# A later first sum of the second routing search, a small load ahead of the token gathers, and a token's place as the smaller of two positions

## Chip, cores, metric

One Trainium2 chip, one of its NeuronCores. The metric is device time of one execution in microseconds (us); lower is better.

## What is computed

Three parts follow one another: windowed attention over 4 x 576 tokens with 8 heads, a mixture-of-experts layer whose router gives each of the 8 experts exactly 288 of the 2304 tokens, and a second layer in which every token goes through all 8 experts, weighted by a balanced (Sinkhorn) table. Cut to what matters here:

```python
def _moe_ref(x, w_gate, w1, w2):
    cap = N // E                                   # 2304 // 8 = 288
    logits = x @ w_gate
    order = np.argsort(-logits.flatten())          # best (token, expert) pairs first
    for idx in order:
        tok, e = (int(idx) // E, int(idx) % E)
        if assigned[tok] >= 0 or counts[e] >= cap:
            continue
        assigned[tok] = e
        counts[e] += 1
    for e in range(E):
        mask = assigned == e
        out[mask] = np.maximum(x[mask] @ w1[e], 0.0) @ w2[e]

def _moe2_ref(x, w_gate, w1, w2):
    P = sinkhorn(np.exp(x @ w_gate - max))         # 8 rounds of row and column sums
    return sum(P[:, e:e + 1] * (np.maximum(x @ w1[e], 0.0) @ w2[e]) for e in range(E))
```

## The kernel before, in words

The program is written in the order in which each engine runs it; waits between engines are put in by the framework. Float32 matrices are split into a high and a low float16 half, and three products (high-high, high-low, low-high) stand for one.

**Routing.** The greedy assignment is done in eight searches (`Router.phase`, one per expert that fills up). A search finds the threshold at which some expert reaches its 288 tokens, six digits of it one after the other. A digit takes these steps: VectorE compares all tokens' scores with up to 64 candidate values (tile `G`, line 504, in two halves); TensorE sums the comparison over the 128 partitions in 18 thin matmuls (line 576); VectorE compares the sums with the room left (`ok`, line 585); TensorE makes a count of `ok` (line 588, "the sum of the digit"); VectorE takes the largest (`cur`, line 590) and forms the next candidates. The search ends in the chosen tokens (`ze`, lines 606 and 607), in an index for the expert's weight rows (`widx`, line 615), in the positions of the chosen tokens (two matmuls, lines 618 and 619, with all-ones and with a triangular matrix `tri`; a running sum `pos`, line 621), and in a list of token numbers: `hot`, two halves of one-hot comparisons (line 640, also named `G` in the trace), 18 thin matmuls (line 671), `idx` (line 676). `books` (lines 654 to 660) takes the filled expert and its tokens out of the scores; line 683 counts what every expert has used.

**Gathers.** `fetched` (GpSimd's queue) gathers the expert's first-layer weight rows by `widx` (line 868), then its 288 token rows from the DRAM tensor `xd` by `idx` into the tile `xg` (line 877, three DMAs), then the second-layer weights. ScalarE makes the high half (line 847) and VectorE the low half (line 838, "the split"). The first layer's splits are called `w1l`, the second layer's `w2l` in the trace; other tiles share these names, so lines tell them apart.

**Main work of stage 1.** For each of the eight experts: transposes of the gathered tokens (line 922), first layer (`l1`, line 907, 8 tiles of 12 matmuls of 288 columns), second layer (line 948, 4 tiles of 24 matmuls; after each, ScalarE and VectorE take it out, lines 952 to 966, which I call the tile's batch), then expert 0 of the second mixture for the tokens so far (`m2_l1`, 96 matmuls of 256 columns, and `m2_l2`). After expert 1 on, a small gate product (`gate2`, line 1287) stands between the second layer and `m2_l1`.

**How searches and main work are laced.** `interleave` runs the main generator and hands over to the search when the nanoseconds that the main work has announced reach what the search asked for (`need`). The search's `yield 1900` is such a request. The first search runs alone, ahead of any expert, with throw-away matmuls (`warm`, line 808) between its digits. The second search is started before the lacing begins: its first digit's comparisons and 18 sums are issued, and the first request of the lacing, `need=1900`, decides where its count (line 588) stands among the first expert's matmuls. Every later request counts from there, so all later places in stage 1 hang on this number.

**Stage 2** (the second mixture's experts 1 to 7) is a long stretch of matmuls that this change does not touch.

Lines of the rows and of the order below are those of the kernel before where the order is of before; in the changed kernel the same statements stand one line higher or up to five lower.

Of the kernel before, what the change touches and what calls it, by code (L numbers as in the profile page):

```python
# [11 lines left out]
F32 = mybir.dt.float32  # L12
F16 = mybir.dt.float16
# [3 lines left out]
OP = mybir.AluOpType  # L17
AX = mybir.AxisListType

B, H, S, D = 4, 8, 576, 64  # L20
N, DM, E, F = 2304, 512, 8, 1024
CAP = N // E
# [356 lines left out]
NC = NT  # L379
STEPS = [6, 5, 5, 5, 5, 6]  # L380
COUNT = 0x4B000000


def step_constants():
# [3 lines left out]
    for n, w in enumerate(STEPS):  # L388
# [9 lines left out]
        if n > 1:  # L398
            u ^= np.uint32(COUNT << (shift + w) & 0xFFFFFFFF)
        out.append(u)  # L400
# [6 lines left out]
def route_tables():  # L407
    p = np.arange(128)
    f = {}
    f["tri"] = -(p[:, None] > p[None, :]).astype(np.float32)  # L410
    c = np.arange(NC)
    base = 128 * c
    val = np.zeros((128, NC, 2), np.float32)
    val[:, :, 0] = base // 64
    val[:, :, 1] = p[:, None]
    f["val"] = val.reshape(128, -1)
    f["iota"] = np.tile(np.arange(1, QB + 1, dtype=np.float32), (128, 1))
    f["code"] = np.tile(8.0 - np.arange(E, dtype=np.float32), (128, 1))
    f["group"] = np.tile(np.arange(3, dtype=np.float32), (128, 1))
    f["wa"] = np.tile(np.array([-DM] * 4 + [-F] * 8, np.float32), (128, 1))  # L420
    f["wb"] = np.concatenate([8 * DM + 128 * np.arange(4)[None] + p[:, None],
                              8 * F + 128 * np.arange(8)[None] + p[:, None]], 1).astype(np.float32)
    cols, n = {}, 0
    for k, a in f.items():
        cols[k] = (n, a.shape[1])
        n += a.shape[1]
    return cols, np.concatenate(list(f.values()), 1)


RC, RTAB = route_tables()  # L430


class Router:
# [96 lines left out]
    def phase(self, ph):  # L530


        nc, wk, Lm = self.nc, self.wk, self.Lm
        V = nc.vector
# [5 lines left out]
        ze = wk.tile([128, 2 * NC], F16, name="ze")  # L540
        if not last:
# [10 lines left out]
            for n, bits in enumerate(STEPS):  # L552
# [7 lines left out]
                elif n:  # L560
                    x = wk.tile([128, 64], I32, name="x")[:, :T]
                    V.scalar_tensor_tensor(x, cur.bitcast(I32).to_broadcast([128, T]), left, base,
                                           op0=OP.logical_shift_left, op1=OP.bitwise_xor)
# [5 lines left out]
                p = self.psum()  # L569
# [7 lines left out]
                if n:  # L577
# [4 lines left out]
                    else:  # L582
                        V.tensor_scalar(base, x[:, 0:1], COUNT, None, op0=OP.bitwise_xor)
                ok = wk.tile([64, E], BF, name="ok")[:T]
# [16 lines left out]
            up = wk.tile([128, NC], F32, name="up")  # L601
# [14 lines left out]
        p = self.psum()  # L616
# [1 line left out]
        nc.tensor.matmul(p[:, :2 * NC], self.ones, ze, start=True, stop=True)  # L618
        nc.tensor.matmul(p[:, 64:64 + 2 * NC], self.tri, ze, start=True, stop=True, skip_group_check=True)
        pos = wk.tile([128, 2 * NC], F32, name="pos")  # L620
        V.tensor_tensor_scan(out=pos, data0=self.one_f, data1=p[:, :2 * NC], initial=0.0, op0=OP.mult, op1=OP.add)
        zv = wk.tile([128, 2 * NC], F32, name="zv")
        V.tensor_add(pos, pos, p[:, 64:64 + 2 * NC])
        V.scalar_tensor_tensor(zv, pos, CAP + 0.5, ze, op0=OP.is_le, op1=OP.mult)
        V.tensor_mul(pos, pos, zv)
        r = wk.tile([128, NC], F32, name="r")
        V.tensor_add(r, pos[:, :NC], pos[:, NC:])
        g = wk.tile([128, NC], F32, name="g")
        V.tensor_scalar(g, r, QB + 0.5, None, op0=OP.is_ge)
        V.scalar_tensor_tensor(g, r, 2 * QB + 0.5, g, op0=OP.is_ge, op1=OP.add)  # L630
# [22 lines left out]
        def books():  # L653
            V.scalar_tensor_tensor(GA, bc(m), cur, A, op0=OP.is_gt, op1=OP.mult)
            V.tensor_scalar(ng, code, wx, -1e30, op0=OP.is_equal, op1=OP.mult)
            V.tensor_sub(self.left, self.left, wx)
            V.tensor_scalar(up, m, cur, -100.0, op0=OP.is_gt, op1=OP.mult)
            V.tensor_add(self.mask, self.mask, up)
            V.scalar_tensor_tensor(self.mask, zv[:, NC:], -100.0, self.mask, op0=OP.mult, op1=OP.add)
            V.tensor_add(Lm, Lm, be(ng))  # L660

        if not last:
# [4 lines left out]
        p = self.psum()  # L667
# [29 lines left out]
SLACK, SL2 = 0.7, 1.06  # L697


def interleave(main, side, slack=lambda: 1.0, drain=True, need=0.0):  # L700


    room = 0.0
    for ns in main:
        room += ns
        while side is not None and room >= need:
            need = next(side, None)
            room = 0.0
            if need is None:
                side = None  # L710
            else:
                need *= slack()
    if side is not None and drain:
        for _ in side:
            pass


class Moe:
# [610 lines left out]

    def stage1(self, ctx, late):  # L1330

        pool = lambda n, b: ctx.enter_context(self.tc.tile_pool(name=n, bufs=b, side="right"))
        x2 = pool("m_x2", 1)
        self.x2 = [x2.tile([128, KT, 2, HN], F16, name="x2" + c) for c in "hl"]
        for i, need in enumerate(self.r.phase(0)):
            if need > 2000:
                self.warm(2)
            if i in (2, 4):
                late.pop(0)()
            if i == 8:  # L1340
                self.load_gate2()

        def routes():
            for ph in range(1, E):
                self.ph = ph
                yield from self.r.phase(ph)
# [9 lines left out]
        side = routes()  # L1356
# [48 lines left out]
                            yield from self.moe1_x(ready)  # L1405
                        yield ns

        interleave(main(), side, lambda: SLACK if self.ph == 1 else SL2, need=1900)

        def last():  # L1410
            x = self.xp.tile([128, 2 * KT, CAP], F16, name="xt", bufs=1).rearrange("p a b -> p (a b)")
# [98 lines left out]
```

## Time and profile before

| what | value |
|---|---|
| runs of the kernel before | 1759.36, 1760.49, 1765.73 us, median 1760.49 us |
| the profiled execution | 1749.37 us |
| its span, first to last instruction | 1747.6 us |
| VectorE busy | 1341.5 us (77%) |
| ScalarE busy | 846.3 us (48%) |
| GpSimd busy | 238.6 us (14%) |
| mean granted TensorE clock over the span | 0.988 |
| chain that ended last | TensorE 61%, issue 10%, VectorE 5%, ScalarE 2% |

PE is TensorE's matmuls, PEld its weight loads, DVE VectorE, ACT ScalarE, POOL GpSimd, SP the engine that issues plain DMAs. A time in brackets at the end of a row is how long the engine had been idle before the instruction, with the engine, tile and line whose end released it; "issue" means that nothing the profile shows was waited for. A clock of 1.00 is 2.4 GHz, 0.50 is 1.2 GHz.

### The profile page before, as it was taken

How to read it: one execution, taken by the hardware profiler on the slowest of the kernel's cores; microseconds unless marked ns; L12 is line 12 of the kernel's file. 1: busy time of each engine (PE TensorE's matmuls, PEld its weight loads, DVE VectorE, ACT ScalarE, POOL GpSimd, SP SyncE). 2: the span in 40 equal slices, each digit the busy share in tenths (PEclk: the TensorE clock that was granted, in tenths of full speed). 3: DMA queues.
4: the chain of work that ended last, by engine and by line, in shares of the span. 5: the costliest groups of instructions: out<-in, count | busy, mean ns of one | idle time of the engine just before them, and what ended most of it. 6: DMA issues, size and time to landing. Idle time of an engine off the chain costs nothing.

```text
span 1747.6 us, 34883 instructions
## 1 busy us (share of the span) xinstructions
PE 1709.8 (98%) x14326; PEld 1280.6 (73%) x14326; DVE 1341.5 (77%) x2572; ACT 846.3 (48%) x1544; POOL 238.6 (14%) x293
## 2 busy tenths in 40 slices
PE   9978999999999999999999999999999999999998
PEld 7956677767777577777777777777777777777777
DVE  6977777766647888878887887888788878886656
ACT  7833443334444455644445543565445544454433
POOL 1323333223410000000000000000000000000111
PEclk9977999999999999999999999999999999999999
DMA  9923444332733144343435235432544334433120
GB/s 330 279 59 110 124 125 134 95 98 77 213 99 102 76 163 154 137 159 112 176 127 209 88 138 211 155 130 89 201 161 157 123 131 155 165 138 148 37 100 37
DMA packets 107568, 241.19 MB, mean 138 GB/s; under 512 B 46384, under 2 KB 72496, under 8 KB 100496
## 3 DMA queue, kind: packets, MB, share of 16 engines
q1 hardware_dynamic: 86768, 151.64, 25.0%
q0 software_dynamic: 20384, 87.05, 14.3%
q8 instruction: 112, 1.84, 0.4%
q14 instruction: 48, 0.39, 0.1%
q10 hardware_dynamic: 256, 0.28, 0.1%
HBM read 173.64 MB, written 61.73 MB: 135 GB/s over the span
## 4 chain that ended last, share of the span: by engine, by line
PE 61%; issue 10%; DVE 5%; ACT 2%; POOL 1%; DMA 0%; POOLq 0%; ACTq 0%; DVEq 0%
PE mm L1176 27%; PE mm L1214 25%; PE mm L907 4%; PE mm L992 3%; PE mm L948 1%; DVE hl L1133 1%; POOL out_dram L1228 1%; ACT raw L1045 0%; DVE w1l L1048 0%; DVE r L1048 0%; DMA raw<-in_w2a_dram,widx 0%; DVE w2l L966 0%; PE r L576 0%; ACT hh L1132 0%; DVE xg L913 0%
## 5 line engine op out<-in xcount | busy, mean ns | idle before, releaser
L1176 PE MATMUL mm<-xb,w1h 128*128 128x384 f16 x2352 | 573.3, 326 | 1.3 <-DVE mm L1147 0.8
L1214 PE MATMUL mm<-w2h,hh 128*128 128x256 f16 x1764 | 480.8, 273 | 0.4 <-DVE t L1238 0.2
L1214 PE MATMUL mm<-w2l,hh 128*128 128x256 f16 x1764 | 480.8, 273 | 0.0
L1214 PE MATMUL mm<-w2h,hl 128*128 128x256 f16 x1764 | 480.8, 273 | 0.0
L1176 PE MATMUL mm<-xb,w1l 128*128 128x384 f16 x1176 | 383.3, 326 | 0.0
L1214 PEld LDWEIGHTS <-hh 128*128 128x128 f16 x3528 | 345.2, 98 | 43.0 <-issue 0.9
L1176 PEld LDWEIGHTS <-w1h 128*128 128x128 f16 x2352 | 230.0, 98 | 154.7 <-issue 6.6
L1214 PEld LDWEIGHTS <-hl 128*128 128x128 f16 x1764 | 172.6, 98 | 20.1
L1133 DVE TENSOR_TENSOR hl<-r,hh 128x1536 f16<-128x1536 f32 x84 | 147.5, 1756 | 41.2 <-ACT hh L1132 41.2
L1176 PEld LDWEIGHTS <-w1l 128*128 128x128 f16 x1176 | 115.0, 98 | 76.1
L1128 ACT ACTIVATE r<-mm 128x384 f32<-128x384 f32 x252 | 119.1, 481 | 100.5 <-PE mm L1176 100.5
L1094 POOL DMA_DIRECT2D ws<-raw x48 | 26.0, 541 | 928.6 <-ACT raw L1045 660.4
L1132 ACT ACTIVATE hh<-r 128x1536 f16<-128x1536 f32 x84 | 124.6, 1483 | 43.6 <-DVE r L1157 41.6
L1139 ACT ACTIVATE mm<-mm 128x384 f32<-128x384 f32 x84 | 40.3, 479 | 175.3 <-PE mm L1176 175.3
L1133 DVE TENSOR_TENSOR hl<-S,hh 128x1152 f16<-128x1152 f32 x84 | 113.5, 1351 | 0.0
L1224 DVE SCALAR_TENSOR_TENSOR acc<-t,P,acc 128x512 f32<-128x512 f32 x126 | 94.7, 752 | 4.5
L907 PE MATMUL mm<-xt,w1h 128*128 128x288 f16 x512 | 97.5, 290 | 0.0
L1132 ACT ACTIVATE hh<-S 128x1152 f16<-128x1152 f32 x84 | 96.4, 1147 | 0.4 <-DVE S L1161 0.4
L1045 ACT ACTIVATE raw<-raw 128x1024 f16<-128x1024 f32 x48 | 50.6, 1055 | 87.3 <-DVE raw L1029 45.8
L912 ACT ACTIVATE w1h<-mm 128x288 f16<-128x288 f32 (+1 forms) x120 | 46.9, 396 | 88.1 <-PE mm L907 87.9
L913 DVE SCALAR_TENSOR_TENSOR w1l<-mm,w1h 128x288 f16<-128x288 f32 (+1 forms) x120 | 50.0, 435 | 45.4 <-ACT w1h L912 45.3
L868 POOL DMA_INDIRECT raw<-in_w2a_dram,widx x64 | 75.9, 1186 | 55.3 <-issue 20.4
(265 smaller groups left out, 2921.5 us busy)
## 6 DMA issues: line engine op xcount, KB each, us to landing
xb<-xw SPq DMA_DIRECT2D x30, 1344.0 KB, 5.9
ws<-raw POOLq DMA_DIRECT2D x48, 448.0 KB, 3.3
ws<-r POOLq DMA_DIRECT2D x48, 448.0 KB, 3.0
raw<-in_w2b_dram SPq DMA_DIRECT2D x32, 512.0 KB, 4.4
raw<-in_w1b_dram SPq DMA_DIRECT2D x56, 256.0 KB, 9.0
w1h<-ws SPq DMA_DIRECT2D x6, 1792.0 KB
w1l<-ws SPq DMA_DIRECT2D x6, 1792.0 KB
w2h<-ws SPq DMA_DIRECT2D x6, 1792.0 KB, 7.2
```

Source lines behind the costliest of these rows:

```text
L868: self.nc.gpsimd.indirect_dma_start(out=r[:, i, :], out_offset=None, in_=rows[lay], in_offset=bass.IndirectOffsetOnAxis(ap=widx[:, c:c + 1 ...
L907: nc.tensor.matmul(p, a[:, k, 128 * f:128 * (f + 1)], rhs(k, b), start=(done[f] == 1 and i == 0), stop=(done[f] == KT and i == 2), skip_gr ...
L912: nc.scalar.activation(h[0][:, f, :n], p, AF.Relu)
L913: nc.vector.scalar_tensor_tensor(h[1][:, f, :n], p, 0.0, h[0][:, f, :n], op0=OP.max, op1=OP.subtract)
L992: nc.tensor.matmul(p, a[:, f, c], b[:, f, :], start=(f == 0 and n == 0), stop=(f == FT - 1 and n == 2))
L1045: self.nc.scalar.activation(hi[:, k], x, AF.Copy, scale=sw)
L1128: nc.scalar.activation(o, p, AF.Relu, scale=SH)
L1132: yield nc.scalar.activation(hq[0][:, i, k], x, AF.Copy)
L1133: yield V.tensor_sub(hq[1][:, i, k], x, hq[0][:, i, k])
L1176: nc.tensor.matmul(p, w[u][:, 2 * j + i // 2, k, 128 * (i % 2):128 * (i % 2 + 1)], x[:, v, r, j], start=(q in (1, 5) and j == 0 and n == 0 ...
L1214: nc.tensor.matmul(p, h[u][:, i, a, 128 * t:128 * (t + 1)], w[v][:, i, b, :], start=(q in (1, 7) and i == 0 and j == 0), stop=(q in (2, 3) ...
L1224: V.scalar_tensor_tensor(self.acc[:, r, :], x, self.P[:, r, e:e + 1], self.acc[:, r, :], op0=OP.mult, op1=OP.add)
```

## The change

Three edits.

- **Place.** `tri` gets -1000 on its diagonal and the running sum starts at 1000, so that a token that isn't chosen has a position above 1000 and a chosen one its own. The place is then the smaller of the two positions (assigned and tied), and two VectorE operations that masked the positions (`zv` and a product) go. In `books`, the mask that used `zv` takes two operations in place of one.
- **Load.** At the seventh step of the first search a DMA on GpSimd's queue reads 38 x 2 single elements of `xd`, spread over the last batch's rows, into a tile `near` that nobody reads. In the built program this load carries the waits for the eight queues of the DMAs that wrote `xd`; the first token gather (line 877) waited for eleven semaphores before, and waits for three after.
- **First request.** `need` goes from 1900 to 3300.

```diff
 def route_tables():
-    f["tri"] = -(p[:, None] > p[None, :]).astype(np.float32)
+    f["tri"] = -(p[:, None] > p[None, :]).astype(np.float32) - FAR * np.eye(128, dtype=np.float32)
...
-        V.tensor_tensor_scan(out=pos, data0=self.one_f, data1=p[:, :2 * NC], initial=0.0, op0=OP.mult, op1=OP.add)
-        zv = wk.tile([128, 2 * NC], F32, name="zv")
+        V.tensor_tensor_scan(out=pos, data0=self.one_f, data1=p[:, :2 * NC], initial=FAR, op0=OP.mult, op1=OP.add)
         V.tensor_add(pos, pos, p[:, 64:64 + 2 * NC])
-        V.scalar_tensor_tensor(zv, pos, CAP + 0.5, ze, op0=OP.is_le, op1=OP.mult)
-        V.tensor_mul(pos, pos, zv)
         r = wk.tile([128, NC], F32, name="r")
-        V.tensor_add(r, pos[:, :NC], pos[:, NC:])
+        V.tensor_tensor(r, pos[:, :NC], pos[:, NC:], op=OP.min)
...
-            V.scalar_tensor_tensor(self.mask, zv[:, NC:], -100.0, self.mask, op0=OP.mult, op1=OP.add)
+            V.tensor_scalar(up, pos[:, NC:], CAP + 0.5, -100.0, op0=OP.is_le, op1=OP.mult)
+            V.tensor_add(self.mask, self.mask, up)
...
+            if i == 6:
+                near = self.xp.tile([38, 2], F16, name="near", bufs=1)
+                xd = self.xd
+                nc.gpsimd.dma_start(near, bass.AP(tensor=xd.tensor, offset=xd.offset + S * (B - 1) * 2 * DM,
+                                                  ap=[[30 * DM, 38], [DM, 2], [1, 1]]))
...
-        interleave(main(), side, lambda: SLACK if self.ph == 1 else SL2, need=1900)
+        interleave(main(), side, lambda: SLACK if self.ph == 1 else SL2, need=3300)
```

What the last edit does to the order, at three places.

TensorE, at the start of the first expert, before. `xg` are the gathered tokens that are transposed, `count` the first sum of the second search, `zero` a throw-away matmul:

```order
L922 LDWEIGHTS xg
L922 MATMUL mm<-id_102,xg 128x96
L588 LDWEIGHTS count
L588 MATMUL r<-ok,count 128x8
L808 LDWEIGHTS zero
L808 MATMUL mm<-zero 128x512
```

The same count in the changed kernel, twelve first-layer matmuls (one tile) later:

```order
L906 LDWEIGHTS w1l
L906 MATMUL mm<-xt,w1l 128x288
L589 LDWEIGHTS count
L589 MATMUL r<-ok,count 128x8
L906 LDWEIGHTS w1h
L906 MATMUL mm<-xt,w1h 128x288
```

The count moved from between the last transpose and the throw-away matmuls to behind the first tile; the later counts of this search follow at the same distances as before (18, then 12 matmuls with the 18 thin sums between), each one tile later.

VectorE, second and third digit of the second search, before. `ok` is the comparison that the digit's count waits for; `w2l<-raw` are the splits of the first expert's second-layer weights, of which there are four, and one stands ahead of the rows shown:

```order
L590 TENSOR_REDUCE cur<-r 128x1
L562 SCALAR_TENSOR_TENSOR x<-cur,base 128x32
L504 TENSOR_TENSOR G<-m,x 128x288 x2
L913 SCALAR_TENSOR_TENSOR w1l<-mm,w1h 128x288
L838 SCALAR_TENSOR_TENSOR w2l<-raw,w2h 128x1024
L581 TENSOR_TENSOR base<-thr,x 128x32
L585 TENSOR_TENSOR ok<-r,rem 32x8
L913 SCALAR_TENSOR_TENSOR w1l<-mm,w1h 128x288
L838 SCALAR_TENSOR_TENSOR w2l<-raw,w2h 128x1024 x2
```

The same place in the changed kernel (two splits stand ahead of it):

```order
L591 TENSOR_REDUCE cur<-r 128x1
L563 SCALAR_TENSOR_TENSOR x<-cur,base 128x32
L505 TENSOR_TENSOR G<-m,x 128x288 x2
L912 SCALAR_TENSOR_TENSOR w1l<-mm,w1h 128x288
L837 SCALAR_TENSOR_TENSOR w2l<-raw,w2h 128x1024 x2
L582 TENSOR_TENSOR base<-thr,x 128x32
L586 TENSOR_TENSOR ok<-r,rem 32x8
```

The third digit's `ok` stood ahead of the third and fourth split and stands now behind all four.

VectorE, end of the second search, before. `G<-md,iota` are the two halves of `hot`, the rows of lines 953 and 958 belong to the third tile of the second layer:

```order
L632 SCALAR_TENSOR_TENSOR md<-g,r 128x18
L953 SCALAR_TENSOR_TENSOR x2l<-mm,x2h 128x2x144
L958 TENSOR_TENSOR w1h<-w2l,mm 128x144
L640 TENSOR_TENSOR G<-md,iota 128x864
L645 TENSOR_TENSOR gm<-g,group 128x54
L647 TENSOR_TENSOR rhs<-val,gm 128x108
L640 TENSOR_TENSOR G<-md,iota 128x864
L654 SCALAR_TENSOR_TENSOR w<-m,cur,A 128x144
```

The same in the changed kernel:

```order
L638 TENSOR_TENSOR G<-md,iota 128x864
L643 TENSOR_TENSOR gm<-g,group 128x54
L645 TENSOR_TENSOR rhs<-val,gm 128x108
L952 SCALAR_TENSOR_TENSOR x2l<-mm,x2h 128x2x144
L959 TENSOR_TENSOR w1h<-mm,w1h 128x144
L960 TENSOR_TENSOR w1l<-mm,w2l 128x144
L961 TENSOR_TENSOR w1l<-mm,w1h 128x144
L965 SCALAR_TENSOR_TENSOR w2l<-w1h,w2h 128x2x144
L965 SCALAR_TENSOR_TENSOR w2l<-w1l,w2h 128x2x144
L638 TENSOR_TENSOR G<-md,iota 128x864
L652 SCALAR_TENSOR_TENSOR w<-m,cur,A 128x144
```

The third tile's rows now stand ahead of the positions, and the fourth tile's batch, which stood behind `books`, stands between the two halves of `hot`. In the third to seventh search every part moves by 9 to 12 matmuls in the same direction: the batch of the second tile goes ahead of `pos`, and line 671 stands behind 18 `m2_l1` matmuls where it stood behind 9.

## Rows read from the trace of the kernel before

**Rows 1.** The page, part 1: busy time, share and instructions of each engine.

```profile
PE 1709.8 (98%) x14326; PEld 1280.6 (73%) x14326; DVE 1341.5 (77%) x2572; ACT 846.3 (48%) x1544; POOL 238.6 (14%) x293
```

**Rows 2.** Windows, PE: length, busy (count), granted clock, DMA share, GB/s.

```profile
149.00:149.50 0.50, 0.50 (x9) 0.70 0.65 107
...
230.00:240.00 10.00, 8.89 (x120) 1.00 0.61 177
```

**Rows 3.** Timeline, end of the first search: start, duration, engine, line, operation.

```profile
128.84 1.20 POOL L868 DMA_INDIRECT raw<-in_w1a_dram,widx  x1 [23.19 <-DVE widx L615]
...
129.24 0.20 DVE L624 SCALAR_TENSOR_TENSOR zv<-pos,ze 128x36 f32<-128x36 f32 x1
...
133.86 0.16 DVE L676 SCALAR_TENSOR_TENSOR idx<-s 96x3 int32<-96x3 f32 x1
...
134.90 0.93 POOL L877 DMA_INDIRECT xg<-xd,idx  x1 [0.98 <-ACT w1h L847]
```

**Rows 4.** Timeline, start of the first expert.

```profile
138.99 4.62 DVE L838 SCALAR_TENSOR_TENSOR w1l<-raw,w1h 128x1024 f16<-128x1024 f32 x4
...
141.43 0.82 PE L922 MATMUL mm<-id,xg 96*128 96x96 f16 x8 [0.18 <-DMA xg<-xd,idx]
...
143.74 0.16 PE L588 MATMUL r<-ok,count 64*128 64x8 bf16 x1 [1.49 <-DVE ok L585]
...
145.08 0.69 PE L907 MATMUL mm<-xt,w1h 128*128 128x288 f16 x2
```

**Rows 5.** Timeline, first layer of the first expert and the splits of its second-layer weights.

```profile
149.36 0.77 PE L576 MATMUL r<-A,G 128*128 128x8 f16 x18
...
155.07 1.06 ACT L847 ACTIVATE w2h<-raw 128x1024 f16<-128x1024 f32 x1 [0.58 <-DMA raw<-in_w2a_dram,widx]
155.12 2.34 DVE L838 SCALAR_TENSOR_TENSOR w2l<-raw,w2h 128x1024 f16<-128x1024 f32 x2
...
156.06 0.17 PE L588 MATMUL r<-ok,count 32*128 32x8 bf16 x1
```

**Rows 6.** Waits of PE from 145 to 600 us: total, times, longest.

```profile
PE r L683 <- DVE P L1287: 5.6, 5, 1.1
...
PE r L618 <- DVE ze L607: 1.2, 1, 1.2
PE r L576 <- DVE G L504: 1.0, 2, 0.7
...
PE r L671 <- DVE G L640: 0.6, 1, 0.6
PE mm L907 <- DVE x2l L953: 0.5, 1, 0.5
```

**Rows 7.** Timeline, end of the third search (the second expert's second layer).

```profile
221.49 0.17 DVE L590 TENSOR_REDUCE cur<-r 128x1 f32<-128x8 f32 x1 [2.17 <-PE r L588]
...
223.02 0.45 DVE L953 SCALAR_TENSOR_TENSOR x2l<-mm,x2h 128x288 f16<-128x288 f32 x1
...
224.21 0.23 DVE L621 TENSOR_TENSOR_SCAN pos<-one_f,r 128x36 f32<-128x36 f32 x1
...
225.88 0.45 DVE L953 SCALAR_TENSOR_TENSOR x2l<-mm,x2h 128x288 f16<-128x288 f32 x1
...
227.87 1.05 DVE L640 TENSOR_TENSOR G<-md,iota 128x864 f16<-128x864 f16 x1
...
229.26 0.45 DVE L953 SCALAR_TENSOR_TENSOR x2l<-mm,x2h 128x288 f16<-128x288 f32 x1
...
230.29 1.05 DVE L640 TENSOR_TENSOR G<-md,iota 128x864 f16<-128x864 f16 x1
...
232.53 0.45 DVE L953 SCALAR_TENSOR_TENSOR x2l<-mm,x2h 128x288 f16<-128x288 f32 x1
...
234.51 0.17 DVE L1287 TENSOR_TENSOR P<-r,P 128x16 f32<-128x16 f32 x1
```

**Rows 8.** Timeline, TensorE at the count of what every expert has used, same search.

```profile
234.73 0.22 PE L683 MATMUL r<-w,ones 128*128 128x144 f16 x1 [1.11 <-DVE P L1287]
```

More of the change, by code (lines that the diff above doesn't have):

```diff
@@ L381 @@
 COUNT = 0x4B000000
+FAR = 1000.0
 def step_constants():
@@ L1330, in stage1 @@
     def stage1(self, ctx, late):
+        nc = self.nc
         pool = lambda n, b: ctx.enter_context(self.tc.tile_pool(name=n, bufs=b, side="right"))
```

## The prediction

> **What bounds the kernel now.** I read first the page's busy times, then the waits of TensorE by releaser, then the granted clock in short windows, then the timeline where the change acts. TensorE is busy 98% of the span [rows 1], so the change can only save what TensorE waits for, or speed up what runs at the low clock. The change acts in stage 1, before 600 us. What TensorE waits for there is little: after 145 us some 11 us in all, of which half is one wait of 1.1 in each of five searches [rows 6]. Ahead of that lies the end of the first search, where TensorE depends on VectorE step by step, with a wait of 1.49 for the count of the second search's first digit [rows 4]. The clock stands at 1.2 GHz there and rises inside the half microsecond from 149.0 (0.70 is a mix of both levels: at 149.3) [rows 2]; before it rises 18 matmuls of 288 columns take 149.36 - 145.08 = 4.28, 0.24 each [rows 4, 5]. After it, 42 of them, two groups of 18 thin sums (0.8 each with the small gap behind) and a count take 156.06 - 149.36 = 6.7 [rows 5], so one takes 0.12.
>
> **The sum is made against the profiled execution, 1749.4 us.** The median of the runs, 1760.5, is 11.1 higher (0.6%); I subtract the same microseconds from it. Less than 0.5%, 8.8 us, is about what a measurement of this kernel can't tell from no change.
>
> **Place.** Two operations go ahead of `idx`, about 0.2 each as `zv` shows [rows 3]; one comes behind it, in `books`, priced as `zv` too. In the first search VectorE is the limit all the way to the second search's candidates: idx comes 0.4 earlier, and what follows `books` 0.2. In later searches the operations lie beside matmuls, and count only where TensorE waits for VectorE, below.
>
> **Load.** GpSimd had nothing to do for 23.19 before the first weight gather [rows 3], and the load sits in that hole: nothing. If it were still in flight there, the weight gather behind it would start later; each microsecond would then move all that hangs on the gathers. What it saves: the token gather started at 134.90, 0.88 after idx was there (133.86 + 0.16), while the weight gather, with one wait, started 0.30 after its releaser (widx; 128.84) [rows 3]. Eight waits fewer are worth between nothing and 0.88 - 0.30 = 0.58. I take 0.4, nearer to the short case, because the remaining three waits are more than one. It pays only the 0.18 that the last transposes waited for that gather [rows 4]; with the 0.2 from VectorE the transposes end 0.2 to 0.4 earlier, I take 0.3.
>
> **First request, at the first expert.** The count no longer stands between the transposes and the first tile, so the 1.49 goes, and the first tile starts 1.5 + 0.3 = 1.8 earlier, near 143.3. But this stall has a successor. The third digit's `ok` stood ahead of the third and fourth split of the second-layer weights and now stands behind all four (the second order pair). The fourth split can't start before ScalarE's copy of that piece, which started at 155.07 after 0.58 of waiting for its gather [rows 5]; that gather's place in the queue hangs on VectorE's first splits from 138.99 on [rows 4], and those move by only 0.2. The two last splits ended at 155.12 + 2.34 = 157.46 [rows 5]; so `ok` comes at 157.46 - 0.2 + 0.3 = 157.5 at best and the count right behind. In the kernel before that count ran at 156.06 with 60 first-layer matmuls done, and the 72nd ended 12 x 0.12 later, at 157.5 [rows 5]. In the changed kernel the count stands behind the 72nd. TensorE, 1.8 ahead, gets there near 155.9 and waits some 1.5. I book 0.1 saved of the 1.8. Bounds: nothing, and the whole 1.8, if the gathers land earlier too.
>
> The clock does not change this: if it rises as early after the start of dense work as before, it moves with the first tile; if it stays at 149.3, half of 1.8 is lost; if it were high from the first tile on, 4.28 / 2 = 2.1 more would be won [rows 4, 5]. In all three TensorE is at that count before 157.5.
>
> **First request, end of the second search.** Three waits of before belong here: 1.2 for ze (line 618), 0.6 for the second half of `hot` (line 671), 0.5 for the fourth tile's low half (line 907); and 1.0 at the next search's first sums (line 576) [rows 6]. Together 3.3. After the change no tile's batch stands between the last count and ze, and TensorE has 15 matmuls (1.8) to do while VectorE takes 1.53 from `cur` to the end of that part [rows 7]: the 1.2 goes. The low half comes before `books`: the 0.5 goes. The second half of `hot` is now late (third order pair). From the last count, with durations of the same operations in the third search [rows 7]: 0.2 to `cur`, 1.53, then 224.21 - 223.02 = 1.19 (third tile), 225.88 - 224.21 - 2 x 0.2 = 1.27 (positions, two operations fewer), 229.26 - 227.87 = 1.39 (first half, `gm`, `rhs`), 234.51 - 232.53 = 1.98 (a tile's batch), 1.05: 8.6. TensorE meanwhile does 54 matmuls (54 x 0.12, a tenth less for the 24 of 256 columns: 6.3) and the first nine sums (0.4), 6.7. So it waits 1.9 where it waited 0.6. At line 576 `books` is late by that wait, but one evacuation fewer stands ahead of the candidates; I take half of the 1.0, bounded by nothing and 1.5. Balance: 3.3 - 1.9 - 0.5 = 0.9 saved, 0 to 2.5.
>
> **First request, third to seventh search.** The wait at line 683 [rows 8] is for the gate product's sum, the last of a VectorE queue that runs `hot`, `books`, fourth tile's batch. TensorE comes to it 9 matmuls later, 9 x 0.11 = 1.0. But VectorE's queue is later as well: the count of the last digit stands 9 first- and second-layer matmuls later (1.1); two operations fewer (-0.4), one more (+0.2), and VectorE no longer idles between `cur`'s part and the second tile's batch as it did (about -0.2). So the queue is 0.6 to 0.7 later against a TensorE 1.0 later, and the 1.1 falls by 0.35, partly as a short wait at line 907 instead. Five times 0.35 is 1.8. The bounds are wide: the whole wait (5.6), or, with VectorE another half microsecond late, 5 x 0.5 = 2.5 the other way.
>
> **Sum.** 0.1 + 0.9 + 1.8 = 2.8 saved: 1746.6 for an execution like the profiled one, and 1760.5 - 2.8 = **1757.7 us** for the median, 0.16%.
>
> **A rule that speaks against it.** The ten microseconds with one of the waits of 1.1 have a granted clock of 1.00 throughout, 2.4 GHz [rows 2]; a wait of 1.9 between thin sums has no row. The Trainium skill, TensorE: Matmul & The Clock Gate, section "HAM oscillation — how this bites in real kernels", says that a TensorE left waiting between groups of matmuls is throttled again, so that the next group starts at the low clock. By that rule the new wait costs more than itself; the trace does not agree for the wait of 1.1. It is the fourth rival below.
>
> **Rivals.**
> 1. *The early lead stays.* If the splits' gathers follow the 0.4 to 0.6 that GpSimd gains, or the third digit's `ok` is not what TensorE waits for, the 1.8 is kept, and the line 683 waits may go wholly: 1.8 + 0.9 + 5.6 = 8.3, some 1752. Against it: the fourth piece was waited for already [rows 5]. Chance 0.2.
> 2. *Everything is given back.* TensorE is no earlier anywhere, since VectorE's queue decides at each place and only changes which line waits; also the case that the load does not do what it says (the three remaining waits cost as much as eleven). 1760 to 1761. For it: VectorE is busy 77% of the span and more at these places [rows 1]. Chance 0.2.
> 3. *Slower: `ok` behind the splits in every expert.* What happens at the third digit of the first expert can happen at each later one: the searches run one tile later against main work, the splits don't, since gathers set them. By the same reckoning the margin there is about 0.4. It decides once the last split ends over 0.4 later than it did against TensorE's place; at the price of the first expert, 1.5 each, five experts cost 7.5, less 2.8: 4.7 slower, 1765. Against it: TensorE waited for `ok` only once, and briefly, after 145. Chance 0.1.
> 4. *The clock falls* at the new wait of 1.9. Before, it rose 5.5 after unbroken work began (143.8 to 149.3) [rows 2, 4]; half of that is lost, 2.7: no change in all. In every search it would be 16, and 1774. Chance 0.02 for either.
>
> **Numbers.** My forecast (saving 1 to 6) has 0.48. The range takes in the forecast, rivals 1 and 2 and half of rival 3, and some spread of the median (1759.4 to 1765.7 for before): 1750.5 to 1764. Faster by over 0.5% needs the upper end of rival 1 or a lucky median: 0.11. Slower by over 0.5%: rivals 3 and 4 with a bad median, 0.05. Within 0.5%: 0.84.
>
> **What would show it.** Right: no wait at the first count; the first matmul of line 907 near 143.3; a wait of 1 to 2 at the third digit's count, released by `ok`, with TensorE level with before at 72 matmuls; the wait at line 618 gone and one of 1.5 to 2 at line 671 in the second search; at line 683 waits of 0.3 to 0.8. Wrong: no wait at the third digit (the lead stays), a clock under 1.00 after 150 us, new waits for `ok` in later experts, or a weight gather of the first search that starts later than 128.84.

## The result, and the profile after

The changed kernel took 1772.8 us (median of 8 runs, 1766.7 to 1780.3), the kernel before 1761.1 beside it (8 runs, 1757.0 to 1765.7). The ratio is **1.0067, 95% interval 1.0043 to 1.0091**: slower, by some 12 us, where 2.8 less were forecast. The profiled execution after took 1769.4 us with a span of 1767.6, against 1749.4 and 1747.6 before.

TensorE did hardly more work; it waited. The page after, busy time, share and instructions of each engine, against [rows 1]:

```profile
PE 1714.5 (97%) x14326; PEld 1281.5 (72%) x14326; DVE 1339.9 (76%) x2563; ACT 843.2 (48%) x1544; POOL 230.3 (13%) x294
```

Waits of TensorE from 145 to 600 us after (total, times, longest), against [rows 6]:

```profile
PE r L589 <- DVE ok L586: 5.5, 4, 2.6
PE r L577 <- DVE G L505: 5.4, 3, 2.6
PE mm L906 <- issue: 2.5, 5, 0.9
PE r L682 <- DVE P L1286: 2.2, 5, 0.4
PE r L670 <- DVE G L638: 1.8, 1, 1.8
...
PE r L589 <- issue: 1.6, 1, 1.6
PE mm L906 <- DVE x2l L952: 0.9, 5, 0.2
```

Half of what was forecast is there: the wait for ze is gone, the second half of `hot` is waited for 1.8 (forecast 1.9), and the wait for the gate product's sum fell from 5.6 to 2.2. But the counts (line 589) and the thin sums (line 577) are waited for 10.9 us, where before it was 1.5. Where does the whole 20 lie? The count of line 682, which runs once per search and five times between 200 and 500 us, cuts the span in three. One line's instructions in that window after (shortest, median and longest in ns, the first and the last start in us):

```profile
L682 PE MATMUL r<-w,ones x5: 223/223/223, 239.3 to 460.2; 128*128 128x144 f16 x5
```

and the same line before, the first of its five being the one of [rows 8]:

```profile
L683 PE MATMUL r<-w,ones x5: 223/223/223, 234.7 to 446.1; 128*128 128x144 f16 x5
```

So up to the first of them the profile after is 4.6 longer, the four searches between first and last take 220.9 in place of 211.4, 9.5 longer, and what follows 5.9.

What are the new waits? The timeline of the first expert after (start, duration, engine, line, operation, idle time before and its releaser):

```profile
149.26 0.77 PE L577 MATMUL r<-A,G 128*128 128x8 f16 x18
...
152.28 0.18 DVE L582 TENSOR_TENSOR base<-thr,x 128x32 int32<-128x32 int32 x1
153.89 0.15 DVE L586 TENSOR_TENSOR ok<-r,rem 32x8 bf16<-32x8 f32 x1 [1.44 <-remote]
154.10 0.16 PE L589 MATMUL r<-ok,count 32*128 32x8 bf16 x1 [2.58 <-DVE ok L586]
```

and of the third expert, at the transposes:

```profile
253.36 0.84 PE L921 MATMUL mm<-id,xg 96*128 96x96 f16 x16
...
254.14 0.17 PE L589 MATMUL r<-ok,count 32*128 32x8 bf16 x1
...
256.10 0.95 POOL L867 DMA_INDIRECT raw<-in_w2a_dram,widx  x1 [0.30 <-issue]
...
256.82 0.81 ACT L922 ACTIVATE xt<-mm 128x768 f16<-128x768 f16 x1 [4.30 <-remote]
...
258.32 0.17 DVE L591 TENSOR_REDUCE cur<-r 128x1 f32<-128x8 f32 x1 [5.66 <-remote]
258.75 0.83 DVE L505 TENSOR_TENSOR G<-m,x 128x288 f16<-128x288 f32 x2
259.26 0.99 PE L577 MATMUL r<-A,G 128*128 128x8 f16 x18 [2.56 <-DVE G L505]
```

In the first, `ok` needs nothing but the 18 thin sums, done at 150.03, and VectorE is free for it at 152.46; it starts at 153.89. In the third, the count ends at 254.31, VectorE is idle, and `cur` starts at 258.32, **4.0 us after what it waits for has ended**; ScalarE's copy of the first eight transposes comes about 3 late too. The row of POOL is the last of eight gathers of this expert's second-layer weights; it ends at 257.05. TensorE itself goes on meanwhile with work that it has, until it needs the answer. I call this a **late post**: TensorE's end of work reaches the other engine late.

The releaser is "remote": the profile names no instruction. But the trace records when a semaphore, the counter by which an engine posts that its work has ended, is moved. TensorE's counter moves at 258.30 here, 0.02 before `cur`. In the first expert it moves three times, at 153.87, 153.94 and 154.02, for work that ended at 150.03, 150.79 and 151.52: the posts pile up and come together, and the engine that waits starts at once. In the profile before, the counter moves a median 0.014 behind the end of TensorE's work. The Trainium skill, Perfetto Trace Analysis, section "Tensor Engine Instruction (MATMUL, LD_WEIGHTS)", says that the profiler's end of a matmul is an estimate, and that the post goes out only when PSUM has acknowledged the data; so the records cannot tell whether the data or the post was held. No step of the prediction had it, and no row of the profile before shows it.

To count them I took some 900 instructions of VectorE and ScalarE whose one wait is on TensorE's counter, and subtracted from each one's start the later of two times: its matmul's end, and the end of the instruction ahead of it. In the profile of before none is over 0.4 us (median -0.08, ends being estimates). After, 22 are, 44.8 us in sum: beside the gathers, and two beside GpSimd's last indirect DMAs. Only TensorE's posts are late: the same reckoning in the same profile for 633 waits that one post of VectorE or ScalarE ends (which one, read from all_fourth below, the same program) finds none over 0.1.

### The profile page after: what moved, and what is told of

The parts are those of the page before. It is cut to its first block, busy times and chain, and to the rows that moved or that the text cites. A ratio compares the mean times of both kernels' runs of the same rounds, so it can differ in the third digit from the quotient of the medians.

```text
span 1767.6 us, 34876 instructions
## 1 busy us (share of the span) xinstructions
PE 1714.5 (97%) x14326; PEld 1281.5 (72%) x14326; DVE 1339.9 (76%) x2563; ACT 843.2 (48%) x1544; POOL 230.3 (13%) x294
## 4 chain that ended last, share of the span: by engine, by line
PE 74%; issue 11%; DVE 9%; ACT 2%; POOL 1%; another core or an unknown queue 1%; DMA 1%; SPq 0%; POOLq 0%; ACTq 0%; DVEq 0%
PE mm L1175 27%; PE mm L1213 25%; PE mm L906 8%; PE mm L991 4%; PE mm L947 3%; PE ps_v L228 2%; PE r L577 1%; PE ps_s L181 1%; DVE hl L1132 1%; PE ps_p L207 1%; POOL out_dram L1227 1%; DVE G L638 1%; DVE w2l L965 1%; PE ps_s L174 1%
## 5 line engine op out<-in xcount | busy, mean ns | idle before, releaser
L906 PE MATMUL mm<-x2l,w0h 128*128 128x256 f16 x288 | 79.2, 275 | 1.8 <-DVE x2l L952 0.9
```

What stands on the lines that cost most here:

```text
L906: nc.tensor.matmul(p, a[:, k, 128 * f:128 * (f + 1)], rhs(k, b), start=(done[f] == 1 and i == 0), stop=(done[f] == KT and i == 2), skip_gr ...
```

## Experiments

Eighteen runs in five sittings, each on one chip with the kernel before beside it. They fall into two kinds, and that is the main finding. In three sittings (**prompt**) the kernel before takes 1752.4 to 1753.2 and no post is late in any kernel; in two (**late**) it takes 1767.7 and 1768.4. The timing above, with before at 1761.1, was of the late kind, while the profile of before that the prediction read is of the prompt kind. The table has, for each run, the ratio to before, the stretch from the first to the last of the five counts of line 682 (before, in its profile: 211.4), and the late posts over 0.4 us.

| run | sitting | ratio, 95% | four searches, us | late posts: sum (count) |
|---|---|---|---|---|
| need_only | prompt | 1.0001 (0.9990-1.0011) | 211.3 | 0 |
| place_load | prompt | 0.9998 (0.9987-1.0008) | 210.0 | 0 |
| place_need | prompt | 0.9983 (0.9974-0.9992) | 210.2 | 0 |
| load_need | prompt | 1.0009 (0.9999-1.0018) | 211.2 | 0 |
| all_fourth (the change) | prompt | 0.9997 (0.9987-1.0008) | 210.3 | 0 |
| before_again | prompt | 1.0002 (0.9991-1.0014) | 210.9 | 0 |
| the change, first timing | late | 1.0067 (1.0043-1.0091) | 220.9 | 44.8 (22) |
| all_again (the change) | late | 1.0043 (1.0029-1.0056) | 229.3 | 52.4 (24) |
| all_third (the change) | late | 1.0045 (1.0030-1.0060) | 228.1 | 50.3 (21) |
| late_splits | late | 1.0068 (1.0053-1.0083) | 222.9 | 47.2 (22) |
| late_splits_all | late | 1.0040 (1.0027-1.0053) | 228.8 | 51.3 (23) |
| place_2600 | late | 1.0053 (1.0036-1.0069) | 223.4 | 50.5 (25) |
| place_only | late | 0.9990 (0.9981-0.9999) | 213.4 | 30.9 (21) |
| plain_w2_after | late | 0.9919 (0.9905-0.9932) | 210.3 | 7.7 (7) |
| plain_w2_before | late | 0.9950 (0.9935-0.9964) | 214.2 | 15.2 (7) |

**Pairs of edits.** First: which edit costs the time? Each of the four has only these edits of the change:

```diff
# need_only: the kernel before, with
-        interleave(main(), side, lambda: SLACK if self.ph == 1 else SL2, need=1900)
+        interleave(main(), side, lambda: SLACK if self.ph == 1 else SL2, need=3300)
# place_load: the changed kernel, with need=1900
# place_need: the changed kernel, without the load of near
# load_need: the kernel before, with need=3300 and the load of near
```

need_only, expected:

> The kernel before with the first request at 3300 and nothing else changed. Theory A (the later first request alone costs the time: the searches run one tile later against splits that gathers set): 1770 to 1775 us, with TensorE waits of 1.5 to 2.6 for ok or G once per expert in experts 1 to 5, as in the changed kernel. Theory B (the small load delays gathers): within 4 us of before, no such waits. Theory C (the place edit is what moves the VectorE queue): within 4 us of before.

place_load, expected:

> The changed kernel with the first request back at 1900: the place edit and the load alone. Theory A: 1757 to 1761 us, no wait over 1.3 in experts 1 to 5 but those of the kernel before. Theory B or C: 1768 or more, with the new waits of 2 to 2.6.

place_need, expected:

> The changed kernel without the load. Theory A: 1770 to 1775, the new waits all there, and the first token gather 0.3 to 0.6 later against idx than with the load. Theory B: 1757 to 1761, the new waits gone.

load_need, expected:

> The changed kernel without the place edit. Theory A: 1770 to 1775. Theory B: 1770 to 1775. Theory C (the place edit, or what it moves on VectorE, costs the time): 1757 to 1761.

None is slower. For a prompt sitting theories A, B and C, each with one edit as the cause, all fall; place and first request together are 3 us faster (0.0017 x 1753). Which edit costs the time in a late one is answered by place_only and place_2600 below.

**The change again, and later splits.** Either the three edits do together what no two do, or the sitting decides. Beside it: are the last splits of the second-layer weights what `ok` waits for (the mechanism of my third rival)?

```diff
# late_splits: place_need, and late_splits_all: the changed kernel, each with
-                    if ph == 0 and i % 6 == 1 and ws[0] is first:
+                    if ph == 0 and i % 6 == 4 and ws[0] is first:
# place_only: the kernel before, with the place edit
```

all_again, unaltered, expected:

> The changed kernel, unaltered, once more. Theory D (the three edits together do what no two of them do: semaphore counts of TensorE seen 2 to 5 us late at VectorE and ScalarE, with waits of 2 to 2.6 in experts 1 to 5): 0.5 to 0.9% slower than before again, the same waits at line 589 and line 577. Theory E (the kernel's own order is harmless, and what was seen came from the execution, not from the program): as the pairs of edits, ratio 0.998 to 1.001, one wait of about 2 for ok at the third digit, one of 1.8 at line 670, five of 0.45 at line 682, and no others over 0.7 between 145 and 540.

late_splits, expected:

> Place and first request, without the load, and the four splits of the first expert's second-layer weights issued three steps later, so that the third digit's ok stands ahead of the last two. If the wait of 2.1 at the third digit is for those splits, it goes: 1.5 to 2.5 us less than place and first request alone, ratio to before 0.997, with the second layer's first matmul not waiting. If it is for something else: the wait stays at 2.

late_splits_all, expected:

> The changed kernel, with the load, and the same later splits. Theory D: slower than before by 0.3 to 0.9%. Theory E: as late_splits to within 2 us.

place_only, expected:

> The place edit alone. By the pairs (first request alone 1.0001, place and first request 0.9983) the place edit saves 2 to 3 us: ratio 0.998 to 0.999. By my prediction's step it is worth 0.2 at the first expert, and 0.2 less at each wait of line 682: ratio 0.9993.

This sitting was a late one. late_splits carries place and first request, as place_need did, without the load: 0.9983 in the prompt sitting and, with splits later, 1.0068 here, where 0.997 was expected. Moving the splits of the first expert does not take the waits of later experts away (2.8 at line 577, twice, in its profile), so the splits are not what makes them. At the third digit of the first expert they are: the count there is waited for 0.68 in all_again, and not at all in late_splits and late_splits_all beside it. The wait that the late posts make, at the second digit, stays: 2.26 in all_again, 2.63 in late_splits_all, 0.81 in late_splits.

place_only, with the order of before, has late posts as well, 30.9 us of them, and is not slower than before in the same sitting. It pays for them all the same, only less: against place_load, a prompt run with the same order on TensorE, its last matmul comes 11.4 later, 10.7 of it lost between 150 and 510 us, the stretch of the gathers. Its waits from 145 to 600 us (in place_load those at line 682 are 4.5, 5, 0.9):

```profile
PE r L682 <- DVE P L1286: 7.1, 5, 1.4
PE r L589 <- DVE ok L586: 2.8, 3, 1.6
PE mm L906 <- ACT xt L922: 2.5, 1, 2.5
PE mm L906 <- issue: 2.3, 3, 1.1
```

**What makes posts late.** The late posts lie beside the gathers. So the second-layer gathers were replaced by plain loads on SyncE's queue; which expert's weights are loaded is then no longer the router's choice.

```diff
+            if lay:
+                src = self.w["a"][1][ph].rearrange("(k p) f -> p k f", p=128)
+                self.nc.sync.dma_start(r, src[:, k:k + per, :])
+                return
             for i in range(per):
                 c = k + i + (0, KT)[lay]
                 self.nc.gpsimd.indirect_dma_start(
```

all_third, unaltered, expected:

> The changed kernel, unaltered, a third time. Theory D (the program's fault, three edits together): 0.4 to 0.7% slower than before wherever it runs. Theory F (it depends on the execution whether TensorE's posts reach VectorE and ScalarE at once or 1 to 6 us late while gathers run, and the order of the change has less slack for late ones): where before runs near 1753 and its posts are prompt, ratio 0.998; where before runs near 1761 to 1768, ratio 1.004 to 1.007 with the waits of 2.6 to 2.8 at line 577.

plain_w2_after, expected:

> The changed kernel with the second-layer weights loaded by plain DMAs on SyncE's queue from the expert of the search's own number, in place of the gathers by widx on GpSimd's queue; so the weights are not the routed expert's. Theory F, with the gathers as what makes posts late: no post later than 0.5 us between 145 and 540 but beside the first-layer gathers, no wait over 1 at line 577, and at least 8 us less than the changed kernel where that has the late posts; about the same where it has not. If posts are late for another reason: the waits of 2.6 stay.

plain_w2_before, expected:

> The kernel before with the same plain loads (the weights are not the routed expert's). Theory F: the changed kernel with plain loads is 1 to 4 us below this one wherever it runs, as the sum of the prediction had it.

place_2600 (place_only with need=2600), expected:

> Place edit with a first request of 2600, no load: the first count a half tile in. A try for a version that beats both: if a half tile keeps some of the gain at line 682 (waits of 0.6 to 0.8 in place of 0.9) and leaves the third digit's count ahead of the transposes, ratio 0.997 to 0.999 wherever it runs; if the third digit falls into the late posts here too, 1.003 or more where posts are late.

A late sitting again, and for the change theory F held. On one chip it took 1777.4 with gathers and 1754.7 without the second layer's, **22.7 us less**. Its late posts fell from 50.3 us to 7.7: five of 0.6 beside the first-layer gathers and two of 2.2 at the very end. Against plain_w2_before, 1760.9, that is 6.2 less, ranges apart (1752.8 to 1756.7 and 1757.5 to 1762.1), where 1 to 4 was expected. This is not the gain of the prediction's sum: plain_w2_before still has five late posts of 2.1, at ScalarE's `x2h` beside the first-layer gathers, where plain_w2_after has 0.6, and the prompt pair below shows no gain. Its wait for the gate product's sum is 1.4 each, 1.1 before:

```profile
PE r L683 <- DVE P L1291: 7.1, 5, 1.4
```

Waits of TensorE in plain_w2_after, 145 to 600 us; none at line 577 is left:

```profile
PE r L682 <- DVE P L1290: 2.2, 5, 0.4
PE r L670 <- DVE G L638: 2.2, 2, 1.8
...
PE r L589 <- DVE ok L586: 0.7, 1, 0.7
```

place_2600, a try for a version that beats both, fell into the late posts like the change. It differs from place_only by the first request alone (2600 for 1900): 1.0053 against 0.9990, in two late sittings. So where posts are late it is the later first request that costs the time, theory A's edit, though not by A's reason.

**With the routed weights, and the change on a prompt chip.** The row offset is read from `widx` into a register of SyncE:

```diff
# dyn_w2_after, dyn_w2_again: the changed kernel; dyn_w2_before: the kernel before; dyn_w_after: lay in (0, 1)
+            if lay in (1,):
+                if lay not in at:
+                    c = (0, KT)[lay]
+                    at[lay] = self.nc.sync.value_load(widx[0:1, c:c + 1], min_val=0, max_val=(E - 1) * (DM, F)[lay])
+                src = rows[lay][bass.ds(at[lay] + 128 * k, 128 * per), :].rearrange("(k p) f -> p k f", p=128)
+                self.nc.sync.dma_start(r, src)
+                return
```

before_again, unaltered, expected:

> The kernel before, unaltered, for its trace where its time is what it was in the timing (1760 and above). Theory F: its span is 10 to 20 us longer than in the profile shown, posts of TensorE reach VectorE and ScalarE up to 3 us late beside the gathers, and most of that is hidden: waits at line 683 of 1.4 in place of 1.1, one of 1 to 2 at line 588, ratio 1.000. Where before runs near 1753: no late post, the waits of the profile shown.

dyn_w2_after, expected:

> The changed kernel with the routed expert's second-layer weights loaded by plain DMAs on SyncE's queue, whose row offset is read from widx into a register. Theory F (gathers make posts late): as plain_w2_after, 0.7 to 0.9% below before where posts are late, no wait over 1 at line 577 of the search; where posts are prompt, ratio 0.997 to 0.999.

dyn_w2_before, expected:

> The kernel before with the same loads by register. Theory F: 0.4 to 0.6% below before where posts are late, and 0.15 to 0.4% above dyn_w2_after: without the gathers the change gains what the prediction's sum had.

dyn_w_after, expected:

> The changed kernel with both layers' weights loaded by plain DMAs with a register offset; only the token rows are still gathered. Theory F: the late posts of 0.6 beside the first-layer gathers go too (ScalarE at line 951), the first-layer weights come earlier, and the time is 0 to 3 us below dyn_w2_after. Against: SyncE's queue holds the loads behind its waits for idx, and the first expert's transposes come later.

all_fourth, unaltered, expected:

> The changed kernel, unaltered. Theory F: on a chip where before runs near 1753 (posts prompt) it is 2 to 4 us faster, ratio 0.998 to 0.999, as the prediction's sum of 2.8 had it, with waits of 2.1 at the third digit, 1.8 at line 670 and 0.45 at line 682 alone; on a chip where before runs above 1760 (posts late) it is 0.4 to 0.7% slower again. Theory D: slower wherever it runs.

dyn_w2_again, expected:

> The changed kernel with the routed second-layer weights loaded by register offset, for a chip of the other kind than the last. Theory F: some 1754 us on either kind, so 0.7 to 0.9% below before and 1.1 to 1.3% below the changed kernel where posts are late, and even with before where they are prompt.

Both sittings were prompt. dyn_w2_after took 1754.1 (ratio 1.0005, 0.9996 to 1.0014), dyn_w2_again 1754.3 (1.0006, 0.9994 to 1.0017), dyn_w2_before 1753.5 (1.0005, 0.9996 to 1.0014): loads by register are even with gathers there, and the changed order gains nothing over the old one, against what was expected of both. That these 1754 stand beside the 1754.7 of the plain loads in a late sitting speaks for a version that takes 1754 on either kind of chip, but the routed loads were never run on a late one: open. dyn_w_after, with both layers' weights on SyncE's queue, is slower, 1.0156 (1.0142 to 1.0169); TensorE waits 2.2 to 8.5 for the first `ok` of a search, in four of them, and 9.0 in the last list. Which of SyncE's waits holds the loads was not followed.

The change itself in a prompt sitting, all_fourth, at the place where the third expert stalled above:

```profile
251.27 0.84 PE L921 MATMUL mm<-id,xg 96*128 96x96 f16 x16
...
251.81 2.22 ACT L922 ACTIVATE xt<-mm 128x768 f16<-128x768 f16 x3 [1.20 <-PE mm L921]
252.04 0.17 PE L589 MATMUL r<-ok,count 32*128 32x8 bf16 x1
...
252.25 0.17 DVE L591 TENSOR_REDUCE cur<-r 128x1 f32<-128x8 f32 x1 [1.83 <-PE r L589]
252.68 0.83 DVE L505 TENSOR_TENSOR G<-m,x 128x288 f16<-128x288 f32 x2
...
254.45 0.77 PE L577 MATMUL r<-A,G 128*128 128x8 f16 x18
```

Same program, same order: `cur` starts with the end of the count (252.21) in place of 4.0 behind it, the releaser has a name, and the sums at 254.45 wait for nothing. Its waits from 145 to 600 us:

```profile
PE r L589 <- DVE ok L586: 3.6, 3, 2.6
PE r L682 <- DVE P L1286: 2.2, 5, 0.4
PE r L670 <- DVE G L638: 1.8, 1, 1.8
...
PE mm L906 <- DVE x2l L952: 0.9, 5, 0.2
...
PE r L577 <- DVE G L505: 0.3, 1, 0.3
```

Theory D (the program's fault wherever it runs) falls. Theory F, that the execution decides, is borne out where posts are late. What it says of the prompt kind is not: 0.9997, an interval from 2.3 us faster to 1.4 slower (0.0013 and 0.0008 of 1753), where it expected 2 to 4 us faster, so a gain is not shown there. Two more things are not shown. The kernel before has no profile from a late sitting; what it pays for late posts is read from place_only, which differs from it by the place edit alone. And whether a chip or its moment makes the kind was not separated: each of the five sittings was on another chip, and within a sitting all runs were alike.

## Why the prediction was wrong, by its own steps

**The step that failed is the one that ties the sum to the runs.** "The median of the runs, 1760.5, is 11.1 higher (0.6%); I subtract the same microseconds from it." The 11 us were not an offset that stays. Some 4 of them lie within the spread of a prompt sitting (median 1753). Most of the rest, as far as place_only tells, is what the order of before pays for late posts, and the change's order pays more. In the sum's own terms, the step from TensorE's end of work to VectorE was put at 0.2 ("0.2 to `cur`") and nowhere at more; in the executions that were timed it was up to 4.4 (4.0 in the rows above), and TensorE waited for it in experts 1 to 5. All six late rows of the table with a later first request and all gathers (the change three times, late_splits, late_splits_all, place_2600) are 0.4 to 0.7% slower; no prompt row is. The new waits for `ok` in later experts were on the prediction's own list of signs that it is wrong. A profile below the fastest of the runs (1749.4 against 1759.4) was a sign that it shows another kind of execution; I noted the gap and argued on.

**Rival 3 was nearest**: slower, by waits of TensorE at the search's digits, once per expert. Its place and size came close (1.5 each forecast, 1.6 to 2.6 in the profile after), and that is luck, since its cause was wrong: not the splits, but posts of TensorE that are late beside the gathers. It had 0.1.

**Place.** Right in kind and, in the searches, in size: line 682 waits 0.90 each in place_load in place of 1.12, the 0.2 of two operations, and the four searches take 210.0 to 210.3 with it, where posts are prompt, against 210.9 to 211.4 without. In the whole time a gain is seen in place_only (0.9990, late) and in place_need against need_only (prompt), but not in place_load (0.9998).

**Load.** Wrong in its reason and in what it saves. I took 0.4 off the start of the token gather for eight waits fewer. Timeline after, GpSimd and VectorE at the end of the first search:

```profile
134.32 0.16 DVE L675 SCALAR_TENSOR_TENSOR idx<-s 96x3 int32<-96x3 f32 x1
...
135.32 0.92 POOL L876 DMA_INDIRECT xg<-xd,idx  x1 [0.92 <-ACT w1h L846]
```

It starts 135.32 - 134.48 = 0.84 after idx, against 0.88 [rows 3]. The trace of before has eight of the eleven waits passed by 128.9, 5 us ahead of idx, so they cost nothing there; what the 0.84 is stays open. With the place edit and no load it is 1.46, since GpSimd's weight gathers end later and the token gather follows them. GpSimd in place_need, where idx ends at 134.96:

```profile
135.17 0.94 POOL L867 DMA_INDIRECT raw<-in_w1a_dram,widx  x1 [0.30 <-issue]
136.42 0.93 POOL L876 DMA_INDIRECT xg<-xd,idx  x1 [0.30 <-issue]
```

From the end of widx the token gather starts after 6.36 in before and in place_need, 6.20 in load_need and 6.02 in the change: place and load together bring 0.34. The transposes did not come earlier for it: they waited 0.2 for that gather in the profile before [rows 4], and 0.6 to 1.8 in 16 of the 19 since, before_again (0.8) among them; the other three (2.2 to 3.1) have place without the load.

**First request, first expert.** Right in kind where posts are prompt: the first count is waited for no more, and the third digit's `ok` makes TensorE wait 1.6 (load_need), 2.1 (need_only, place_need) or 2.6 (all_fourth); I had 1.5. So the lead is given back there, with up to 1.1 more. The rows of all_fourth have the mechanism as I gave it, `ok` behind the fourth split and that behind ScalarE's copy:

```profile
158.19 1.23 DVE L837 SCALAR_TENSOR_TENSOR w2l<-raw,w2h 128x1024 f16<-128x1024 f32 x1 [1.51 <-ACT w2h L846]
...
159.43 0.15 DVE L586 TENSOR_TENSOR ok<-r,rem 32x8 bf16<-32x8 f32 x1
...
159.63 0.16 PE L589 MATMUL r<-ok,count 32*128 32x8 bf16 x1 [2.56 <-DVE ok L586]
```

**End of the second search.** Right: the wait at line 618 gone, 1.76 at line 670 (1.9 forecast), the rest 0.2 to 0.3.

**Third to seventh search.** The wait fell by more than I said, 1.12 to 0.45 in place of 0.75, but little of it is time saved. With the new first request alone the four searches are no shorter (211.3 against 210.9 and 211.4), since 0.43 each appear at the fourth tile's low half; with place as well they are 0.7 to 1.2 shorter, 0.2 to 0.3 a search where I had 0.35. This, and the token gather, is why the prompt gain is nearer 0 than 2.8.

**Rival 4, the clock.** The Trainium skill, TensorE: Matmul & The Clock Gate, section "HAM oscillation — how this bites in real kernels", has TensorE throttled again by waits between groups of matmuls. After the wait of 1.8 at line 670 the clock fell in 5 of 13 profiles with that wait, the one after the timing among them, and not in the other 8 (all_fourth is one): the rule holds sometimes, for the same wait. Windows after: length, busy (count), granted clock, DMA share, GB/s:

```profile
183.00:186.40 3.40, 3.40 (x19) 0.50 0.97 285
312.70:316.10 3.40, 3.20 (x10) 0.50 0.42 134
```

Each such stretch at 1.2 GHz loses half of its 3.4, so these two cost 3.4 of the 20. I had given it 0.02. In late sittings, with waits of 2 to 4, the clock fell after some of these too, and it is a large part of the price. In all_third (span 1775.0, all_fourth's 1749.9), besides one stretch at 184.5:

```profile
208.40:211.80 3.40, 3.40 (x14) 0.50 0.07 29
263.00:266.40 3.40, 3.40 (x12) 0.50 0.01 2
317.60:324.40 6.80, 6.41 (x39) 0.50 0.15 48
433.70:437.10 3.40, 3.40 (x12) 0.50 0.00 0
```

All five lose some 10 us; all_fourth has one stretch of 3.4 after 150 us, which loses 1.7.

**A reading.** TensorE's waits in the profile before from 145 to 600 us add to 12.9, not some 11; no term hangs on it.

## What to carry to other kernels

If the profile's time lies outside the range of the runs, it shows an execution of another kind; find out what the missing time is before adding and subtracting microseconds from it, because a change in order may pay for it again. A chain of short steps between engines is best laid where TensorE has other work to cover a post that comes microseconds late, above all beside indirect gathers; an order that uses the slack up to the last tenth, as this one, wins nothing where posts are prompt and loses where they are not. And an effect of half a per cent is tested on more than one chip, and at more than one time, before its sign is believed.

## What the runs showed of the hardware

- In some sittings, while GpSimd's gathers run, work that TensorE has ended is seen by VectorE and ScalarE up to 5.8 us late (`cur` at 316.79 against a count ended at 310.98, in all_again), in others never over 0.4. VectorE's and ScalarE's own posts are never over 0.1 late in the same profile. The gathers themselves take as long in both: mostly 0.95 on GpSimd each, 1.25 apart. Replacing second-layer gathers by plain loads removed the late posts beside them.
- In the late profiles fewer semaphore updates are recorded (12,754 after, 14,443 before), which is why many releasers read "issue"; "remote" stands where the update is recorded, but far behind any matmul's end. Whether the same thing that loses records delays posts is open.
- Loads whose row offset comes from a register on SyncE's queue were even with gathers by index list for the second layer (1.0005), and cost 1.6% when the first layer's stood in the same queue.
